# Output layer of one token block by seven half-size products for eight, with the retention stretches before it moved forward

## The chip, the cores and the metric

The kernel runs on one core of one Trainium2 chip. The metric is the device time of one execution in microseconds (us). Three runs of the kernel before gave a median of 314.52 us (314.04 to 317.05). The engines are named as in the profile: PE is TensorE's matmul side and PEld its weight load, DVE is VectorE, ACT is ScalarE, POOL is GpSimd, SP is SyncE, which here only issues DMAs.

## The reference

Two operators in a row. Retention over q, k and v of shape (batch 8, heads 8, sequence 576, head width 64), and a bilinear feed-forward layer on its output, with 4608 tokens of width 512 and an inner width of 1536:

```python
scores = scale * np.matmul(q, k.transpose(0, 1, 3, 2))
Dmat = np.where(rel >= 0, gamma[:, None, None] ** rel[None, :, :], 0.0)
attn = np.matmul(scores * Dmat[None], v)
x = attn.transpose(0, 2, 1, 3).reshape(B * S, H * D)
out = (x @ w_a) * (x @ w_b) @ w_out
```

Inputs and output are float32. The kernel multiplies in bfloat16 and sums in float32.

## The kernel before, in words

**Blocks.** The 4608 tokens go through the feed-forward layer in blocks of 512, 256, 256 and then seven of 512. A block has twelve hidden tiles F of 128 columns. For each F, `ffn_block` (line 1288) forms `pa` = x w_a (line 1324) and `pb` = x w_b (line 1345) in PSUM, four matmuls each; ACT copies `pa` to SBUF as `ha` (line 1338), DVE multiplies it with `pb` into the hidden tile `hT` (line 1350), which is called the gate here. When all twelve are there, the output layer `hT` w_out follows. The blocks from token 2048 on use seven products for eight in the hidden layer too (`middle_layer`, `last_layer`), which the change leaves alone.

**The two forms of the output layer.** The plain one (line 1371): for each of the four groups of 128 tokens, twelve matmuls of 512 columns into one PSUM tile `po`, then a copy by ACT or DVE to an output tile, put on the list `held`; `store_held` issues the DMA at a set place. The other form is `rows_mixed` (line 932), used by every block from token 1536 on: it splits rows, inner width and columns in two and needs seven half-size products for eight. Its 84 matmuls of 256 columns (line 972) read `hT`, `wo_sb`, the precomputed weight sums `wo_sums` (15 instructions of `weight_sums`, line 876) and row sums `hsum`, which DVE forms from `hT` (`row_sums`, line 889): five instructions over F 0 to 7, five over F 8 to 11; two of each five update `hT` in place. Its partial results lie in PSUM tiles `m340`, `m341`, `m15` (two banks, that of the retention's output tile `o`) and `m52`. ACT copies some of them (`straight`, `crossed`, line 984), POOL and DVE add them up (lines 996, 1006, 1013), and the next block stores them (`store_formed`, `store_mixed`). The order of the products is: ways 3 and 4 (24 matmuls), way 1 (12), then `cross` of the first half (12), which uses `m15`, `cross` of the second (12), which uses `m52`, and ways 6 and 7 (24).

**Retention.** It runs beside the feed-forward layer in units called pairs, 256 tokens each, numbered 0 to 17; pair n must be done before the block that reads its tokens. For a pair, SP loads q, k, v (`load_pair`, line 163), POOL casts and scales them (`ahead`, line 489), SP issues two transposing DMAs (`turn`, line 550) into `qkT`, and a `stretch(into, outof)` (line 772) puts on PE: outputs from the states of pair `outof`, the state sums `kv` of pair `into` (two PSUM banks of the pool `ps_ffn`, which has four and which `pa`, `pb`, `po` and the `m` tiles share), the scores of `into`, and the rest of the outputs of `outof`. The additions that free `kv` go to DVE (line 616), the copies of states and outputs to ACT (lines 619 to 627, 759). In the changed kernel's order on DVE the additions of an even pair stand behind the row sums that were issued before its stretch.

**Places.** The order is written by hand: the list `todo` (from line 1651) holds pairs of a place and a function; places count 512-column matmuls of the feed-forward layer, and a function is issued at the first edge (after a whole F, mostly) at or behind its place. `starts[n]` is the place at which the block of pair n begins. Small DVE jobs wait in `jobs` with a priority and are issued a few per F; ACT copies wait in `copies_due` and `later`. The block of tokens 1024 to 1535 begins at place 288 in both kernels. `MADE` holds the places of eight weight combinations (`combine`, line 1082) for the hidden layer of later blocks.

**Memory.** `stage` holds two buffers for each of q, k and v; a third for pairs 2, 5 and 8 lies in the pool `begin`, which is closed when the pools of `rows_mixed` (`hsum`, `straight`, `crossed`, `less`) open. `BY_HALVES` (line 1285) names six `pa` groups whose matmuls run as two of 256 columns.

Of the kernel before, what the change touches and what calls it, by code (L numbers as in the profile page):

```python
# [18 lines left out]
def kernel(  # L19
# [66 lines left out]
    h_pool = pool("hT", 1)  # L86
    ha_pool = pool("ha", 6)
    o_pool = pool("osb", 4)
    late, early = {}, ExitStack()
    begin = early.enter_context(tc.tile_pool(name="begin", bufs=1))  # L90
    ctx.push(early)

    def pools_mixed():

        if not late:
            early.close()
            for name, bufs in (("hsum", 1), ("straight", 2),
                               ("crossed", 2), ("less", 2),
                               ("combo", 1), ("rows", 1)):
                late[name] = early.enter_context(  # L100
                    tc.tile_pool(name=name, bufs=bufs))

# [979 lines left out]
    def combine(p, m, i):  # L1082

        pools_mixed()
        if (p, m) not in combos:
            shape = [128, 4, 2, 2, 128]
            if p in COMMON:
                both = late["combo"].tile([128, 2] + shape[1:], BF16,
                                          tag="combo", name="combos")
                combos[p, 0], combos[p, 1] = both[:, 0], both[:, 1]  # L1090
            else:
                combos[p, m] = stage.tile(shape, BF16, tag=("qf", "kf")[m],
                                          name="combo")
            for own in (0, 1):
                if (p, own) in combos:
                    combos[p + 1, own] = combos[p, own]
        (a11, a12), (a21, a22) = quarter_weights(m, p, 2)
        s3, s1, s2, s4 = (combos[p, m][:, k] for k in range(4))
        out, one, other, op = [(s3, a11, a21, ALU.subtract),
                               (s1, a21, a22, ALU.add),  # L1100
                               (s2, a22, s3, ALU.subtract),
                               (s4, a12, s2, ALU.subtract)][i]
        def made():
            nc.vector.tensor_tensor(out, one, other, op=op)

        jobs.append((1.5 + i / 10, 0.5, made))
# [2 lines left out]

    def combine_rows(tok0, i):  # L1110
        if tok0 not in row_combos:
            row_combos[tok0] = late["rows"].tile([128, 4, 2, 256], BF16,
                                                 tag="rows", name="rows")
# [136 lines left out]
    def last_layer(tok0, xT, hT, sums):  # L1250
# [31 lines left out]
            work(SHARE[way])  # L1282
        work(math.inf, 1)

    BY_HALVES = [(1024, F) for F in (4, 5, 6)] + [
        (256 * MIXED, F) for F in (8, 9, 10)]

    def ffn_block(tb, tok0, n, runs):

        xT = x_of(tok0, n)  # L1290
        hT = h_pool.tile([128, NF, 512], BF16, tag="h", name="hT")
        if tok0 >= 256 * MIXED:
            pools_mixed()
            sums = late["hsum"].tile([128, 3, NF // 2, 2, 128], BF16, tag="hsum",
                                  name="hsum")
# [9 lines left out]
        for count in runs:  # L1305
# [35 lines left out]
            for F in range(f0, f0 + count):  # L1341
# [8 lines left out]
                nc.vector.tensor_tensor(hT[:, F, 0:n], has[F][:, 0:n],  # L1350
                                        pb[:, 0:n], op=ALU.mult)
# [9 lines left out]
            f0 += count  # L1361
        if tb == 0:
            yield from rows_together(tok0, hT, (0, 1))
        if tok0 >= 256 * MIXED:
# [238 lines left out]
    for n in blocks:  # L1603
        for i in range(tok // 256, (tok + n) // 256):
            starts[i] = at
        at += total(n, tok >= 256 * MIXED) - 4 * (tok in MIDDLE)
        tok += n

    def early_casts():
# [34 lines left out]
    def third_turn():  # L1644
        for w in (Q, K):
            turned((4, w), (5, w))
        for i in (4, 5):
# [12 lines left out]
    todo += [(170, stretch, (3, None)), (201, stretch, (4, 3)),  # L1660
             (217, spread, ()),
             (252, stretch, (5, 4)), (274, open_alone, (5,)),
             (278, close_outputs, (5,)), (336, stretch, (6, None)),
             (372, stretch, (7, 6)), (408, stretch, (8, 7))]
    for n in range(8, NP, 2):
        todo += [(starts[n] - (92 if n == 16 else 116 if n > 8 else 112), stretch, (n + 1, n)),
                 (starts[n] - 52, stretch, (n + 2, n + 1))
                 if n + 2 < NP else
                 (starts[n] - 60, close_alone, (n + 1,))]
    placed = {args[0]: at for at, fn, args in todo if fn is stretch}  # L1670
# [3 lines left out]
             10: 412.2}  # L1674
    todo += [(116.1, load_pair, (4, (K, V))), (116.3, load_pair, (5,)),
             (141.5, load_pair, (6,)), (200.1, load_pair, (7, (Q, K))),
             (200.3, load_pair, (7, (V,))), (253.2, load_pair, (8, (Q,))),
             (253.3, store_held, (1,)), (253.4, load_pair, (8, (K,))),
             (253.5, store_held, (1,)), (253.6, load_pair, (8, (V,))),
             (253.7, store_held, (1,)), (283.2, load_pair, (9, (Q,))),  # L1680
             (283.3, store_held, (1,)), (283.4, load_pair, (9, (K, V))),
             (345, load_pair, (10, (Q,))), (380.1, load_pair, (10, (K,))),
             (380.2, store_held, (1,)), (380.3, load_pair, (10, (V,))),
             (380.4, store_held, (1,)), (411.9, load_pair, (11, (Q,))),
             (411.95, store_held, (2,)), (412.3, load_pair, (11, (K, V))),
             (458, load_pair, (12,)), (447, store_held, (2,)),
             (456, store_held, (2,))]
    NOW = 1, 4
    LATE = 30, 50, 8
    CAST_A, TURN_A, CAST_B, TURN_B = 96, 58, 96, 58  # L1690
# [51 lines left out]
```

## Time and profile before

| | |
|---|---|
| median of three runs | 314.52 us (314.04 to 317.05) |
| profiled execution | 313.77 us |
| its span | 312.1 us |
| PE busy | 301.7 us |
| DVE, POOL, ACT busy | 225.1, 201.9, 156.0 us |
| block of tokens 1024 to 1535 on PE | 85.86 to 120.44 us |
| block of tokens 1536 to 2047 on PE | 120.44 to 153.06 us |

The span is the time from the first to the last instruction of the profiled execution; the rest of its time lies around it. All times in the text are from the span's start. In a timeline row stand the start, the duration of the group, the engine, the line, the operation with its tiles (out<-in), and the count; in a group's row stand the busy time and the mean in ns of one. Matmuls overlap, so a group's duration includes the last one's way through the array: the pace is read from the starts. A few matmul records are missing from the trace; a group of 23 or 3 where the code issues 24 or 4 is such a case.

### The profile page before, as it was taken

How to read it: one execution, taken by the hardware profiler on the slowest of the kernel's cores; microseconds unless marked ns; L12 is line 12 of the kernel's file. 1: busy time of each engine (PE TensorE's matmuls, PEld its weight loads, DVE VectorE, ACT ScalarE, POOL GpSimd, SP SyncE). 2: the span in 40 equal slices, each digit the busy share in tenths (PEclk: the TensorE clock that was granted, in tenths of full speed). 3: DMA queues.
4: the chain of work that ended last, by engine and by line, in shares of the span. 5: the costliest groups of instructions: out<-in, count | busy, mean ns of one | idle time of the engine just before them, and what ended most of it. 6: DMA issues, size and time to landing. Idle time of an engine off the chain costs nothing.

```text
span 312.1 us, 9647 instructions
## 1 busy us (share of the span) xinstructions
PE 301.7 (97%) x3926; PEld 199.5 (64%) x3957; DVE 225.1 (72%) x452; ACT 156.0 (50%) x348; POOL 201.9 (65%) x288
## 2 busy tenths in 40 slices
PE   6899999999999999999999999999999999999995
PEld 2654457768555554567864787468746875687774
DVE  5944355768757685779777986888579968877873
ACT  6746346626435454555456545544635454335530
POOL 3980089675996679963799769985998350035413
PEclk9999999999999999999999999999999999999999
DMA  7999999998998999999999486837704020012004
GB/s 235 268 183 204 255 261 193 183 218 202 189 171 217 232 229 191 250 235 269 201 283 216 93 215 175 200 82 170 223 4 70 30 106 2 2 57 82 1 2 134
DMA packets 144797, 50.97 MB, mean 163 GB/s; under 512 B 126576, under 2 KB 141680, under 8 KB 144752
## 3 DMA queue, kind: packets, MB, share of 16 engines
q1 hardware_dynamic: 138272, 45.10, 63.3%
q0 software_dynamic: 5808, 4.72, 9.8%
q8 instruction: 31, 0.51, 0.7%
q10 hardware_dynamic: 672, 0.52, 0.5%
q14 instruction: 14, 0.11, 0.1%
HBM read 37.75 MB, written 9.44 MB: 151 GB/s over the span
## 4 chain that ended last, share of the span: by engine, by line
PE 91%; DMA 3%; DVE 2%; issue 1%; SPq 0%; POOL 0%; ACT 0%; POOLq 0%; DVEq 0%; ACTq 0%
PE m L972 16%; PE pb L1345 13%; PE pa L1324 12%; PE pb L1209 9%; PE pa L1209 9%; PE po L1371 8%; PE lm L1152 7%; PE ls L1152 3%; PE la L1152 2%; DMA wa_sb<-in_moe_w_a_dram 2%; PE po L858 2%; DMA vf<-in_v_dram 2%; PE sc L660 2%; PE o L688 1%; PE kv L589 1%
## 5 line engine op out<-in xcount | busy, mean ns | idle before, releaser
L1350 DVE TENSOR_TENSOR hT<-ha,pb 128x512 bf16<-128x512 bf16 (+1 forms) x60 | 34.5, 577 | 32.1 <-PE pb L1345 27.9
L1345 PE MATMUL pb<-xT,wb_sb 128*128 128x512 bf16 (+1 forms) x235 | 49.8, 335 | 0.4
L1324 PE MATMUL pa<-xT,wa_sb 128*128 128x256 bf16 (+1 forms) x252 | 47.7, 318 | 0.4 <-issue 0.3
L996 POOL TENSOR_TENSOR osb<-crossed,straight 128x256 f32<-128x256 f32 x24 | 17.5, 758 | 46.6 <-ACT crossed L984 46.6
L1338 ACT CAST ha<-pa 128x512 bf16<-128x512 f32 (+1 forms) x60 | 29.8, 500 | 35.4 <-PE pa L1324 34.2
L1324 PEld LDWEIGHTS <-wa_sb 128*128 128x128 bf16 x256 | 24.5, 98 | 16.0 <-DVE sums L616 0.2
L1345 PEld LDWEIGHTS <-wb_sb 128*128 128x128 bf16 x240 | 23.4, 98 | 17.1 <-issue 0.3
L541 POOL TENSOR_TENSOR vb<-vf,vs 128x512 bf16<-128x512 f32 x30 | 31.5, 1071 | 1.2
L1209 PE MATMUL pb<-xT,wb_sb 128*128 128x512 bf16 x125 | 32.1, 379 | 0.2
L1209 PE MATMUL pa<-xT,wa_sb 128*128 128x512 bf16 x119 | 31.4, 379 | 0.7 <-issue 0.3
L504 POOL TENSOR_TENSOR qkb<-qf,qs 64x512 bf16<-64x512 f32 x24 | 25.0, 1057 | 10.5 <-issue 4.7
L972 PEld LDWEIGHTS <-hT 128*128 128x128 bf16 x288 | 28.1, 98 | 5.0 <-DVE hT L906 0.5
L1219 ACT CAST ha<-pa 128x512 bf16<-128x512 f32 x32 | 18.7, 585 | 24.8 <-PE pa L1209 24.8
L1222 DVE TENSOR_TENSOR hT<-ha,pb 128x512 bf16<-128x512 bf16 x32 | 21.9, 684 | 10.4 <-PE pb L1209 6.7
L534 POOL CAST qkb<-kf 64x256 bf16<-64x256 f32 x60 | 27.3, 481 | 1.5
L1371 PE MATMUL po<-wo_sb,hT 128*128 128x512 bf16 x113 | 26.7, 379 | 0.8 <-issue 0.6
L509 POOL TENSOR_TENSOR qkb<-qf,qs 64x512 bf16<-64x512 f32 x24 | 26.1, 1107 | 0.7
L972 PE MATMUL m<-wo_sums,hsum 128*128 128x256 bf16 x216 | 25.7, 273 | 0.0
L530 POOL CAST qkb<-kf 64x512 bf16<-64x512 f32 x30 | 20.8, 694 | 5.0 <-DMA kf<-in_k_dram 3.6
L906 DVE TENSOR_TENSOR hsum<-hT 128x512 bf16<-128x512 bf16 (+2 forms) x51 | 23.1, 484 | 0.5
L972 PEld LDWEIGHTS <-hsum 128*128 128x128 bf16 x216 | 21.1, 98 | 2.5
L1209 PEld LDWEIGHTS <-wb_sb 128*128 128x128 bf16 x128 | 12.3, 98 | 14.3
(165 smaller groups left out, 577.3 us busy)
## 6 DMA issues: line engine op xcount, KB each, us to landing
qf<-in_q_dram SPq DMA_DIRECT2D x32, 256.0 KB, 4.5
vf<-in_v_dram SPq DMA_DIRECT2D x32, 256.0 KB, 4.3
kf<-in_k_dram SPq DMA_DIRECT2D x31, 256.0 KB, 4.2
out_dram<-osb SPq DMA_DIRECT2D x9, 512.0 KB, 3.6
out_dram<-osb SPq DMA_DIRECT2D x22, 128.0 KB, 2.7
wo_sb<-in_moe_w_out_dram POOLq DMA_DIRECT2D x3, 512.0 KB, 16.0
out_dram<-osb SPq DMA_DIRECT2D x6, 256.0 KB, 3.9
wa_sb<-in_moe_w_a_dram POOLq DMA_DIRECT2D x2, 512.0 KB, 8.3
```

The lines of the kernel that those rows point to most:

```text
L504: nc.gpsimd.tensor_tensor(per_head(qkb[0:64, Q])[:, hs], per_head(t[0:64])[:, hs], by[0:64, hs].unsqueeze(2).to_broadcast([64, H, D]), op= ...
L509: nc.gpsimd.tensor_tensor(per_head(qkb[64:128, Q])[:, 1 - r::2], per_head(t[64:128])[:, r::2], by[64:128, r::2].unsqueeze(2).to_broadcast( ...
L534: nc.gpsimd.tensor_copy(to[:, :, 1 - r], fro[:, :, r])
L541: nc.gpsimd.tensor_tensor(vb[:, e].rearrange("p (h d) -> p h d", d=D), t[:, e].rearrange("p (h d) -> p h d", d=D), decay[:, at], op=ALU.mult)
L972: nc.tensor.matmul(to, rows, cols, start=(begins and p == 0), stop=True, skip_group_check=True)
L1152: nc.tensor.matmul(to[:, m], w[:, c], x[:, c], start=(way in (1, 2, 5) and m == c == 0), stop=True, skip_group_check=True)
L1209: nc.tensor.matmul(p1, w[:, c, F * 128:F * 128 + 128], xT[:, c], start=(c == 0), stop=(c == NC - 1))
L1324: nc.tensor.matmul(pa[:, at:at + width], wa_sb[:, c, fs], xT[:, c, at:at + width], start=(c == at == 0), stop=(c == NC - 1), skip_group_ch ...
L1338: nc.scalar.copy(ha[:, 0:n], pa[:, 0:n])
L1345: nc.tensor.matmul(pb[:, 0:n], wb_sb[:, c, fs], xT[:, c], start=(c == 0), stop=(c == NC - 1))
L1350: nc.vector.tensor_tensor(hT[:, F, 0:n], has[F][:, 0:n], pb[:, 0:n], op=ALU.mult)
L1371: nc.tensor.matmul(po, hT[:, F, u * 128:(u + 1) * 128], wo_sb[:, F], start=(F == 0), stop=(F == NF - 1))
```

## The change

The output layer of the block of tokens 1024 to 1535 takes the form of `rows_mixed`: the tests on `256 * MIXED` (1536) become tests on `SQUARE` (1024). `store_mixed` gets a branch for pairs below 6, whose tokens lie in their natural order, and issues two DMAs of 128 rows for each. Since the pools of `rows_mixed` open 144 places sooner, the third staging buffers move from `begin` to a pool of their own, `extra`, which later also holds the combinations for which the pools `combo` and `rows` were opened. The stretches of pairs 6, 7 and 8 move from places 336, 372 and 408 to 316, 344 and 380, that of pair 10 from 52 to 48 places ahead of its block, in a block that is 6 places shorter; the loads and stores around them are put in another order, and `MADE` moves back. `BY_HALVES` becomes empty. On PE, stretch 6 now follows F = 3 of the block (before: F = 5), stretch 7 follows F = 6 (before: F = 10), stretch 8 follows F = 11 (before: half of the output layer), and stretch 10 follows F = 11 of its block (before: F = 10).

```diff
+    SQUARE = 1024
...
+    extra = pool("extra", 1)
...
-                               ("crossed", 2), ("less", 2),
-                               ("combo", 1), ("rows", 1)):
+                               ("crossed", 2), ("less", 2)):
...
-        extra = n < MIXED + 3 and n % 3 == 2
-        return (begin if extra else stage).tile(
+        third = n < MIXED + 3 and n % 3 == 2
+        return (extra if third else stage).tile(
...
         for kp, r0, m, b, s0 in rows_of(n):
+            if n < MIXED:
+                on.dma_start(out[b * S + s0:b * S + s0 + m, :], osb[:, kp])
+                continue
...
-    MADE = [385 + 8 * i for i in range(8)]
+    MADE = [400 + 9 * i for i in range(8)]
...
-            if p in COMMON:
-                both = late["combo"].tile([128, 2] + shape[1:], BF16,
-                                          tag="combo", name="combos")
...
+            combos[p, m] = combos[p + 1, m] = (
+                extra if p in COMMON else stage).tile(
+                    shape, BF16, tag=("qf", "kf")[m], name="combo")
...
-    BY_HALVES = [(1024, F) for F in (4, 5, 6)] + [
-        (256 * MIXED, F) for F in (8, 9, 10)]
+    BY_HALVES = []
...
-        if tok0 >= 256 * MIXED:
+        if tok0 >= SQUARE:
             pools_mixed()
...
-        if tok0 >= 256 * MIXED:
+        if tok0 >= SQUARE:
             yield from rows_mixed(tok0, hT, sums)
...
-             (278, close_outputs, (5,)), (336, stretch, (6, None)),
-             (372, stretch, (7, 6)), (408, stretch, (8, 7))]
+             (278, close_outputs, (5,)), (316, stretch, (6, None)),
+             (344, stretch, (7, 6)), (380, stretch, (8, 7))]
...
-                 (starts[n] - 52, stretch, (n + 2, n + 1))
+                 (starts[n] - (52 if n > 8 else 48), stretch, (n + 2, n + 1))
...
-             (200.3, load_pair, (7, (V,))), (253.2, load_pair, (8, (Q,))),
-             (253.3, store_held, (1,)), (253.4, load_pair, (8, (K,))),
-             (253.5, store_held, (1,)), (253.6, load_pair, (8, (V,))),
-             (253.7, store_held, (1,)), (283.2, load_pair, (9, (Q,))),
-             (283.3, store_held, (1,)), (283.4, load_pair, (9, (K, V))),
+             (200.3, load_pair, (7, (V,))), (253.05, load_pair, (8, (Q,))),
+             (253.3, load_pair, (8, (K, V))),
+             (283.2, store_held, (2,)), (283.3, load_pair, (9, (Q,))),
+             (283.4, store_held, (2,)), (283.5, load_pair, (9, (K, V))),
```

More of the change, by code (lines that the diff above doesn't have):

```diff
@@ L1086, in combine @@
             shape = [128, 4, 2, 2, 128]
-            if p in COMMON:
-                both = late["combo"].tile([128, 2] + shape[1:], BF16,
-                                          tag="combo", name="combos")
[L1090 to L1096, printed above, removed]
+            combos[p, m] = combos[p + 1, m] = (
+                extra if p in COMMON else stage).tile(
+                    shape, BF16, tag=("qf", "kf")[m], name="combo")
         (a11, a12), (a21, a22) = quarter_weights(m, p, 2)
@@ L1111, in combine_rows @@
         if tok0 not in row_combos:
-            row_combos[tok0] = late["rows"].tile([128, 4, 2, 256], BF16,
-                                                 tag="rows", name="rows")
+            row_combos[tok0] = extra.tile([128, 4, 2, 256], BF16,
+                                             tag="vf", name="rows")
         x = x_of(tok0, 512)
@@ L1363, in ffn_block @@
             yield from rows_together(tok0, hT, (0, 1))
-        if tok0 >= 256 * MIXED:
+        if tok0 >= SQUARE:
             yield from rows_mixed(tok0, hT, sums)
@@ L1605 @@
             starts[i] = at
-        at += total(n, tok >= 256 * MIXED) - 4 * (tok in MIDDLE)
+        at += total(n, tok >= SQUARE) - 4 * (tok in MIDDLE)
         tok += n
@@ L1676 @@
              (141.5, load_pair, (6,)), (200.1, load_pair, (7, (Q, K))),
-             (200.3, load_pair, (7, (V,))), (253.2, load_pair, (8, (Q,))),
-             (253.3, store_held, (1,)), (253.4, load_pair, (8, (K,))),
-             (253.5, store_held, (1,)), (253.6, load_pair, (8, (V,))),
-             (253.7, store_held, (1,)), (283.2, load_pair, (9, (Q,))),
-             (283.3, store_held, (1,)), (283.4, load_pair, (9, (K, V))),
-             (345, load_pair, (10, (Q,))), (380.1, load_pair, (10, (K,))),
[L1683 to L1687, printed above, removed]
+             (200.3, load_pair, (7, (V,))), (253.05, load_pair, (8, (Q,))),
+             (253.3, load_pair, (8, (K, V))),
+             (283.2, store_held, (2,)), (283.3, load_pair, (9, (Q,))),
+             (283.4, store_held, (2,)), (283.5, load_pair, (9, (K, V))),
+             (345, load_pair, (10, (Q,))), (380.1, load_pair, (10, (K,))),
+             (380.2, store_held, (2,)), (380.3, load_pair, (10, (V,))),
+             (380.4, store_held, (2,)), (411.9, load_pair, (11, (Q,))),
+             (412.3, load_pair, (11, (K, V))),
+             (452, load_pair, (12,))]
     NOW = 1, 4
```

## The prediction

> **What bounds the kernel now.** I read the page first: TensorE's share, its granted clock, the chain that ended last.
>
> ```profile
> span 312.1 us, 9647 instructions
> ...
> PE 301.7 (97%) x3926; PEld 199.5 (64%) x3957; DVE 225.1 (72%) x452; ACT 156.0 (50%) x348; POOL 201.9 (65%) x288
> ...
> PEclk9999999999999999999999999999999999999999
> ...
> PE 91%; DMA 3%; DVE 2%; issue 1%; SPq 0%; POOL 0%; ACT 0%; POOLq 0%; DVEq 0%; ACTq 0%
> ```
>
> TensorE is busy for 97% of the span at full clock and holds 91% of the chain. Then I asked for the busy times in three stretches: the block of tokens 1024 to 1535, the block of 1536 to 2047, and the rest.
>
> ```profile
> 85.86:120.44 34.58, 34.16 (x466) 18.05 (x468) 23.60 (x43) 17.37 (x34) 26.09 (x35) 1.00 1.01 206
> 120.44:153.06 32.62, 32.30 (x437) 20.97 (x440) 25.36 (x45) 15.52 (x30) 22.83 (x30) 1.00 1.07 235
> 153.06:312.10 159.04, 154.00 (x1904) 109.83 (x1915) 122.33 (x251) 76.75 (x157) 98.99 (x128) 1.00 0.44 110
> ```
>
> The columns are the stretch, its length, then busy time of PE, PEld, DVE, ACT and POOL. In the two blocks that the change touches PE idles for 0.42 and 0.32 us. So the time moves one for one with TensorE's work there, and there is next to no wait to win back.
>
> **The change part by part.** First the products of the last layer of the block of 1024, from the timeline of PE (start, duration, operation):
>
> ```profile
> 108.70 5.34 PE L1371 MATMUL po<-wo_sb,hT 128*128 128x512 bf16 x24
> ...
> 115.47 5.13 PE L1371 MATMUL po<-wo_sb,hT 128*128 128x512 bf16 x23 [0.16 <-issue]
> 120.44 1.03 PE L1324 MATMUL pa<-xT,wa_sb 128*128 128x512 bf16 x4
> ```
>
> The last layer of the block of 1536, from the busy times of line 972 alone (the stretch, its length, PE and PEld):
>
> ```profile
> 143.86:153.06 9.20, 9.20 (x84) 8.10 (x83) 1.00 1.12 194
> ```
>
> Starts, not durations, give the pace. The second `po` group runs 4.97 us to 120.44 and shows 23 products: 0.216 us each, and one record of 24 is missing (the "issue" gap of 0.16 is that record, no idle time). The block's 48 full-width products therefore take 48 x 0.216 = 10.37 us, and the retention stretch between them takes (120.44 - 108.70) - 10.37 = 1.37. The block of 1536 already does the new form: 84 products of 256 columns in 9.20 us without a gap, 0.1095 each. **The saving is 10.37 - 9.20 = 1.17 us.** The Trainium skill, "TensorE: Matmul & The Clock Gate", section "Back-to-back issue gap", speaks against it: a stream of weight loads and matmuls is to sustain about 131 ns per matmul at 512 columns and 81 at 128, so that a half width costs far more than half; by it, with some 98 ns (an estimate between the two) at 256, 48 x 0.131 = 6.3 us would become 84 x 0.098 = 8.2, a loss of 1.9 us. The rows above, 216 and 110 ns, don't agree with it.
>
> Next the products in halves (`BY_HALVES`): three in each of the two blocks.
>
> ```profile
> 91.04 1.03 PE L1324 MATMUL pa<-xT,wa_sb 128*128 128x512 bf16 x4
> 91.91 1.03 PE L1345 MATMUL pb<-xT,wb_sb 128*128 128x512 bf16 x4
> 92.77 1.04 PE L1324 MATMUL pa<-xT,wa_sb 128*128 128x256 bf16 x8
> 93.64 1.03 PE L1345 MATMUL pb<-xT,wb_sb 128*128 128x512 bf16 x3
> ...
> 96.34 0.45 PE L589 MATMUL kv<-vb,qkb 64*64 64x64 bf16 x32
> ...
> 96.98 1.05 PE L1324 MATMUL pa<-xT,wa_sb 128*128 128x256 bf16 x8
> 97.86 1.03 PE L1345 MATMUL pb<-xT,wb_sb 128*128 128x512 bf16 x3
> ```
>
> A full product group takes 91.91 - 91.04 = 0.87, one in halves 0.87 to 0.88; six cost 0.06 us too much at most. **Saving 0.06.**
>
> Moving the stretches of pairs 6, 7 and 8 forward changes no PE work. But it places stretch 8 (and 10, by the 48 for 52) directly behind the last hidden product of its block and ahead of the 84 products. The sums that these products need are made on VectorE, and here lies the one wait that I find. Stretch 8 takes two of the four PSUM banks (`kv0`, `kv1`); the two after them go to `m340`, `m341`; the seventh tile, `m52`, gets kv0's bank, and its first product waits until VectorE has added kv0 up. That addition stands in VectorE's queue behind the row sums:
>
> ```profile
> L1350 DVE TENSOR_TENSOR hT<-ha,pb 128x512 bf16<-128x512 bf16 x36 | 24.6, 686 | 26.6 <-PE pb L1345 25.1 <-ACT ha L1338 1.5
> L906 DVE TENSOR_TENSOR hsum<-hT 128x1024 bf16<-128x1024 bf16 x12 | 10.9, 904 | 0.3
> L906 DVE TENSOR_TENSOR hT<-hT 128x1024 bf16<-128x1024 bf16 x8 | 7.0, 912 | 0.0
> L906 DVE TENSOR_TENSOR hsum<-hT 128x512 bf16<-128x512 bf16 x21 | 7.8, 416 | 0.0
> L906 DVE TENSOR_TENSOR hT<-hT 128x512 bf16<-128x512 bf16 x14 | 5.4, 416 | 0.0
> L613 DVE COPY sums<-kv 128x256 f32<-128x256 f32 x5 | 2.1, 413 | 0.0
> L616 DVE TENSOR_TENSOR sums<-kv,sums 128x256 f32<-128x256 f32 x44 | 18.6, 422 | 1.6
> ```
>
> Let T be the end of the last hidden product (block start 85.86, 24 groups of 4 x 0.216, stretch 6 at 96.98 - 96.34 = 0.6 or a little more, stretch 7 as long as stretch 8: about 108.6). VectorE then does in order, by the mean durations: the gate 0.686, one wide sum 0.904, two wide updates 1.824, three sums 1.248, two updates 0.832, the copy 0.413 and two additions 0.844: T + 6.75. PE comes to `m52` after stretch 8 (1.37) and 48 products (5.26): T + 6.63. I take a **wait of 0.12 us**. The ends: 0, since back to back these operations start up to a tenth closer than they last; and 2.2, if all three wide ones take their longest and the gate before (line 10 of 12) is late:
>
> ```profile
> L906 DVE TENSOR_TENSOR hsum<-hT x51: 276/416/1345, 136.6 to 302.1; 128x512 bf16<-128x512 bf16 x21, 128x256 bf16<-128x256 bf16 x18, 128x1024 bf16<-128x1024 bf16 x12
> L906 DVE TENSOR_TENSOR hT<-hT x34: 279/416/1527, 141.7 to 302.5; 128x512 bf16<-128x512 bf16 x14, 128x256 bf16<-128x256 bf16 x12, 128x1024 bf16<-128x1024 bf16 x8
> ```
>
> That is 0.44 + 2 x 0.61 more than the means. The late gate I estimate at 0.5: ScalarE's state copies of stretch 7 come to stand just ahead of the copy that the gate of F = 10 needs, and two of them last this long:
>
> ```profile
> 109.60 1.24 ACT L619 CAST states<-sums 64x512 bf16<-64x512 f32 x2
> ```
>
> In the block of 1536 one wide update, not two and a wide sum, stands behind the last gate, so kv0 is free 0.904 + 0.912 sooner, 1.7 us before `m52`: no wait.
>
> What is new beside it costs nothing so long as its cover holds.
>
> ```profile
> L1104 DVE TENSOR_TENSOR combos<-wa_sb,combos 128x512 bf16<-128x512 bf16 x2 | 1.8, 908 | 0.0
> L996 POOL TENSOR_TENSOR osb<-crossed,straight 128x256 f32<-128x256 f32 x24 | 17.5, 758 | 46.6 <-ACT crossed L984 46.6
> 128.40 2.04 POOL L541 TENSOR_TENSOR vb<-vf,vs 128x512 bf16<-128x512 f32 x2
> ```
>
> VectorE gains ten row sums in the first block (6.6 us by the means above) and hands weight combinations (`MADE`), of 0.9 us at most, to the next; the windows leave it 11.0 and 7.3 us idle. ScalarE makes four copies for two and is idle for half the window. POOL gains four additions of 0.76 us, which lie between the casts of pairs 9 and 10, so that those of pair 10 end at 130.4 + 3.0 = 133.5. Stretch 10 needs them at T + 1.4 + 9.3 + 20.7 + 1.4, about 141.4; if that cover went, PE would wait us for us. The held output copies go; the block's stores are still four of 256 KB, issued by the next block; `extra` takes over the third staging buffers and the combinations, with the reuse that they had.
>
> The moved stretches need their transposed queries and keys sooner. From the SP and POOL timelines and the transposes' time to landing:
>
> ```profile
> 82.83 3.62 SPq L558 DMA_TRANSPOSE qkT<-qkb  x2
> 86.50 1.74 SPq L171 DMA_DIRECT2D vf<-in_v_dram  x2
> 88.72 4.41 SPq L558 DMA_TRANSPOSE qkT<-qkb  x2
> ...
> 103.16 1.35 SPq L558 DMA_TRANSPOSE qkT<-qkb  x1
> ```
>
> ```profile
> 91.12 0.75 POOL L534 CAST qkb<-kf 64x256 bf16<-64x256 f32 x2
> ```
>
> ```profile
> DMA to landing us min/median/max: 2.7/3.6/7.1
> ```
>
> Stretch 6 now starts after line 3, at 85.86 + 8 x 0.864 = 92.8; its transposes are issued by 86.5 and, at the median, have landed by 90. Stretch 7 starts after line 6, at 92.8 + 0.7 + 5.2 = 98.7; its second transpose waits for the cast that ends at 91.9, is issued by 93.1 even with the one load that now goes ahead, and lands by about 96.7. Stretch 8 starts at 108.6; its transposes, issued at 103.16 and after, move ahead of the stores, so not later, and land by about 108. The slack is 2 us at the first two and about 1 at the third: no cost. SP then issues eight stores around pair 9's query load where two stood behind it, which puts its keys and values about 1 us later; stretch 9 comes 1.1 us sooner but more than 17 us after T.
>
> The sum: -1.17 - 0.06 + 0.12 = **-1.11 us**. The profiled execution took 313.77 us (span 312.1 and 1.67 around it), so 312.66; it lay 0.75 below the median of the three runs, 314.52, and on that median the forecast is **313.4**.
>
> **The rivals.**
>
> 1. *VectorE holds the bank (slower).* The row sums run beside POOL's multiplications for pair 9, and `m52` waits 2.2 us instead of 0.12: -1.23 + 2.2 = +0.97, 315.5. It decides from a wait of 1.23 us, that is, the second addition on kv0 ending after T + 7.9. For it: the two longest L906 rows, which are twice the means. Against: POOL stands idle until pair 9's queries land, about when the updates run. The Trainium skill, "SBUF — State Buffer", section "Who interferes with whom", has it that a VectorE instruction with two SBUF inputs and a GpSimd one that reads SBUF exclude each other for a whole instruction; the spread of 0.68 to 1.53 us for the same 1024-wide sums agrees with that.
>
> 2. *A transpose is late.* If one of stretch 7 takes the longest landing, 7.1 us, and the load ahead of it adds 1 us, it lands at 93.1 - 1.25 + 7.1 + 1.0 = 99.95, 0.7 after PE wants it: -1.11 + 0.7, 314.1. The neighbours' rows, at 3 to 4 us, speak against it.
>
> 3. *The change doesn't do what it says*: 84 half-width products cost in this block what 48 full ones do, 0.123 each. That gives 314.5 and is refuted next door, unless weights read from fresh sums load slower here.
>
> 4. *More is won*: no wait at `m52`, and 0.3 of the 0.74 us of idle time goes too: -1.53, 313.0.
>
> **How the numbers follow.** Forecast 0.66; rival 1 0.14; rival 2 0.09; rival 3 0.04; rival 4 0.07. The range starts at the fastest run shown, 314.04, less 1.53, 312.5, and ends at rival 1, 315.5. Within 1% (3.1 us, what a measurement of this kernel can tell from no change) lie all cases: 0.94. Faster by over 1% would need 2 us more than all work that goes: 0.02. Slower by over 1% needs rivals 1 and 2 together at several times their price: 0.04.
>
> **What would show it.** In the changed profile the block from its first `pa` should take 34.6 - 1.1 = 33.5 us, with 84 `m` products at 0.11 us and one gap of 0 to 0.3 us ahead of the 49th, released by VectorE's additions. No idle time of PE should be released by a transpose at stretches 6 to 8. The block of 1536 should shrink by 0.03 and everything behind 153 stay as it was, only 1.1 us earlier. The prediction is wrong if that gap exceeds 1 us, if PE waits for `qkT`, if `m` products run slower than 0.11 us, or if the later blocks wait for POOL's shifted casts.

## The result and the profile after

The changed kernel takes 317.12 us (median of nine runs, 316.35 to 319.33) where the kernel before takes 314.81 beside it (314.04 to 317.05). The ratio is 1.0083 with a 95% interval of 1.0060 to 1.0107: slower by about 2.6 us. Forecast was a gain of 1.1. Ratios here and below leave out executions in which the chip was disturbed, so they are not the quotients of the medians. The profiled execution took 317.05 us; its page first:

```profile
span 315.3 us, 9724 instructions
...
PE 304.6 (97%) x3969; PEld 201.2 (64%) x3969; DVE 237.3 (75%) x466; ACT 156.8 (50%) x350; POOL 206.3 (65%) x292
...
PE 84%; DVE 7%; DMA 3%; ACT 2%; issue 1%; SPq 0%; POOL 0%; DVEq 0%; ACTq 0%; POOLq 0%
```

PE's share of the chain falls from 91 to 84% and DVE's rises from 2 to 7%. (PE's busy time can't be compared: this trace lacks fewer matmul records.) The same three stretches as before, cut at the first matmul of each block (length, busy time of PE, PEld, DVE, ACT, POOL):

```profile
85.86:123.13 37.27, 34.35 (x494) 20.34 (x493) 29.95 (x49) 18.34 (x36) 29.09 (x37) 1.00 1.07 206
123.13:156.28 33.15, 32.76 (x430) 19.87 (x428) 30.50 (x55) 15.43 (x30) 24.64 (x32) 1.00 1.05 230
156.28:315.30 159.02, 155.01 (x1918) 109.85 (x1915) 122.64 (x251) 76.75 (x157) 99.04 (x128) 1.00 0.43 108
```

Everything ahead of 85.86 and behind token 2048 lasts as long as before (159.02 and 159.04). The loss is in the two blocks: 37.27 for 34.58 and 33.15 for 32.62, together +3.22 us. PE's timeline shows where:

```profile
107.90 1.03 PE L1341 MATMUL pb<-xT,wb_sb 128*128 128x512 bf16 x4
...
110.42 2.79 PE L976 MATMUL m<-wo_sums,hT 128*128 128x256 bf16 x24
113.05 1.04 PE L976 MATMUL m<-wo_sums,hsum 128*128 128x256 bf16 x8
115.31 0.61 PE L976 MATMUL m<-wo_sums,hsum 128*128 128x256 bf16 x4 [1.22 <-DVE hsum L907]
115.76 0.60 PE L976 MATMUL m<-wo_sb,hT 128*128 128x256 bf16 x4
117.13 1.14 PE L976 MATMUL m<-wo_sb,hT 128*128 128x256 bf16 x8 [0.77 <-DVE hT L907]
119.20 1.47 PE L976 MATMUL m<-wo_sb,hT 128*128 128x256 bf16 x12 [0.93 <-DVE sums L617]
120.51 2.78 PE L976 MATMUL m<-wo_sums,hsum 128*128 128x256 bf16 x24
123.13 1.03 PE L1320 MATMUL pa<-xT,wa_sb 128*128 128x512 bf16 x4
...
128.00 1.02 PE L1341 MATMUL pb<-xT,wb_sb 128*128 128x512 bf16 x4 [0.39 <-DVE hT L1346]
```

T, the end of the last hidden product, is 107.90 + 4 x 0.216 = 108.76. The 84 products run from 110.42 to 123.13, 12.71 us, and PE stands still three times: for the row sums that way 1 still lacks, for the updates of `hT` that follow them, and for the addition that frees `m52`'s bank. Read from the starts the three gaps come to 3.5 us (the listed waits, 2.92, count from modelled ends). Without them the products would take 12.71 - 3.5 = 9.2 us, as forecast. Stretch 8 lasts 110.42 - 108.76 = 1.66 where it lasted 1.37. A fourth wait stands at the third `pb` of the next block. What PE waits for is all on VectorE:

```profile
109.12 0.68 DVE L1346 TENSOR_TENSOR hT<-ha,pb 128x512 bf16<-128x512 bf16 x1
109.72 1.44 DVE L907 TENSOR_TENSOR hsum<-hT 128x1024 bf16<-128x1024 bf16 x1
111.08 2.98 DVE L907 TENSOR_TENSOR hT<-hT 128x1024 bf16<-128x1024 bf16 x2
113.99 2.55 DVE L907 TENSOR_TENSOR hsum<-hT 128x512 bf16<-128x512 bf16 x3
116.46 1.36 DVE L907 TENSOR_TENSOR hT<-hT 128x512 bf16<-128x512 bf16 x2
117.75 0.41 DVE L614 COPY sums<-kv 128x256 f32<-128x256 f32 x1
118.27 1.34 DVE L617 TENSOR_TENSOR sums<-kv,sums 128x256 f32<-128x256 f32 x3
```

VectorE works without a pause from the last gate on and does what the prediction lists, in that order, but the second of the last three additions ends at about 119.1, T + 10.4 and not T + 6.75. The gate, the copy and the additions take their usual times. The eight row sums don't. POOL at the same time:

```profile
109.57 2.48 POOL L505 TENSOR_TENSOR qkb<-qf,qs 64x512 bf16<-64x512 f32 x2 [5.22 <-PE o L689]
112.11 2.86 POOL L510 TENSOR_TENSOR qkb<-qf,qs 64x512 bf16<-64x512 f32 x2
```

It stands idle for 5.22 us until 109.57 and then multiplies for pair 9, just when the row sums begin to take about twice their time. (The two wide sums of 106.68 and 108.52, while POOL was idle, took 0.68 us.)

### The profile page after: what moved, and what is told of

Its sections match the earlier page's. It is cut to its first block, busy times and chain, and to the rows that moved or that the text cites. A ratio compares the mean times of both kernels' runs of the same rounds, so it can differ in the third digit from the quotient of the medians.

```text
span 315.3 us, 9724 instructions
## 1 busy us (share of the span) xinstructions
PE 304.6 (97%) x3969; PEld 201.2 (64%) x3969; DVE 237.3 (75%) x466; ACT 156.8 (50%) x350; POOL 206.3 (65%) x292
## 4 chain that ended last, share of the span: by engine, by line
PE 84%; DVE 7%; DMA 3%; ACT 2%; issue 1%; SPq 0%; POOL 0%; DVEq 0%; ACTq 0%; POOLq 0%
PE m L976 16%; PE pb L1341 12%; PE pa L1320 11%; PE pa L1206 9%; PE pb L1206 9%; PE lm L1149 7%; PE po L1367 5%; PE ls L1149 3%; DVE hsum L907 2%; DVE hT L907 2%; DMA wa_sb<-in_moe_w_a_dram 2%; PE la L1149 2%; PE po L859 2%; PE sc L661 1%; DMA vf<-in_v_dram 1%
## 5 line engine op out<-in xcount | busy, mean ns | idle before, releaser
L1000 POOL TENSOR_TENSOR osb<-crossed,straight 128x256 f32<-128x256 f32 x28 | 20.1, 746 | 49.5 <-ACT crossed L988 45.1
L1320 PE MATMUL pa<-xT,wa_sb 128*128 128x512 bf16 (+1 forms) x232 | 48.2, 335 | 0.0
L976 PEld LDWEIGHTS <-hT 128*128 128x128 bf16 x336 | 32.4, 98 | 7.7 <-DVE hT L907 1.7
L1341 PEld LDWEIGHTS <-wb_sb 128*128 128x128 bf16 x240 | 23.4, 98 | 18.8 <-issue 1.0
L1320 PEld LDWEIGHTS <-wa_sb 128*128 128x128 bf16 x232 | 22.2, 98 | 17.1 <-DVE sums L617 0.5
L976 PE MATMUL m<-wo_sums,hsum 128*128 128x256 bf16 x252 | 30.1, 273 | 1.2 <-DVE hsum L907 1.2
L907 DVE TENSOR_TENSOR hsum<-hT 128x512 bf16<-128x512 bf16 (+2 forms) x57 | 29.3, 546 | 0.5
L976 PEld LDWEIGHTS <-hsum 128*128 128x128 bf16 x252 | 24.6, 98 | 4.3 <-DVE hsum L907 1.5
L976 PE MATMUL m<-wo_sb,hT 128*128 128x256 bf16 x168 | 20.2, 273 | 1.9 <-DVE hT L907 1.0
L1149 PEld LDWEIGHTS <-combo 128*128 128x128 bf16 x192 | 18.8, 98 | 4.7
```

The costliest lines, as they stand in the source:

```text
L907: lambda e=ways[i]: nc.vector.tensor_tensor(*e[:3], op=e[3]))
L976: nc.tensor.matmul(to, rows, cols, start=(begins and p == 0), stop=True, skip_group_check=True)
L1149: nc.tensor.matmul(to[:, m], w[:, c], x[:, c], start=(way in (1, 2, 5) and m == c == 0), stop=True, skip_group_check=True)
L1320: nc.tensor.matmul(pa[:, at:at + width], wa_sb[:, c, fs], xT[:, c, at:at + width], start=(c == at == 0), stop=(c == NC - 1), skip_group_ch ...
L1341: nc.tensor.matmul(pb[:, 0:n], wb_sb[:, c, fs], xT[:, c], start=(c == 0), stop=(c == NC - 1))
```

## The experiments

Three theories are tried. The names e1 to e11 are those that the expectations use; the changed kernel's second run is a1. **A**: the row sums, which read two operands from SBUF, are slowed by POOL's work for pair 9. **B**: VectorE's queue behind the last gate is too long by itself. **C**: the moved stretches and loads cost the time. All variants start from the changed kernel. Profiled executions differ by up to 1.8 us in the part ahead of the block of 1024, which is nearly the same code in all (it begins at 85.64 to 87.41), so profiles are compared from the block's start: "two blocks" is from there to the first product of the block of 2048. The changed kernel itself takes 70.42 us there in one profile and 70.04 in the next, so single profiles can't tell apart differences of 0.4 us.

**The changed kernel once more, beside other runs (a1).**

> The changed kernel as it is, on the chip and beside the runs of the following three. All theories: ratio to the kernel before 1.006 to 1.011; 12.7 us from the first of the 84 products to the end of the block; wide row sums of 1.4 to 1.5 us beside POOL's multiplications for pair 9.

Ratio 1.0103 (1.0074 to 1.0132), waits of 0.62, 0.78 and 0.92, two blocks 70.04 us, 12.1 us for the 84 products and not 12.7. The loss and its place repeat; the waits' sizes differ by some tenths between executions.

**Pair 9's query load behind all eight stores (e1).**

```diff
-             (283.2, store_held, (2,)), (283.3, load_pair, (9, (Q,))),
-             (283.4, store_held, (2,)), (283.5, load_pair, (9, (K, V))),
+             (283.2, store_held, (2,)), (283.3, store_held, (2,)),
+             (283.4, load_pair, (9, (Q,))), (283.5, load_pair, (9, (K, V))),
```

> Edit: the query load of pair 9 is issued on SP behind all eight held stores and no longer between them, so that POOL's ten instructions for pair 9 start some 3 us later, at about 112.5 us. Theory A (the row sums on DVE are slowed because POOL's pair 9 runs beside them): those row sums that now end before POOL starts take 0.68 us (1024 wide) and 0.42 us (512 wide), the three waits of PE inside the 84 products (3.5 us by the starts) fall below 1.2 us in sum, the kernel takes about 314.8. Theory B (DVE's queue behind the last gate is too long by itself): the waits stay where they are with 3 us or more, about 317. Theory C (the moved stretches and loads cost it, whatever the products): about 317 as well.

Ratio 1.0055 (1.0029 to 1.0080). PE still waits 1.72 and 0.93 us (3.1 in sum by the starts), and the two blocks take 70.02 us, no less than in a1. VectorE's and POOL's timelines of this kernel:

```profile
110.80 1.29 DVE L907 TENSOR_TENSOR hT<-hT 128x1024 bf16<-128x1024 bf16 x2
112.00 3.63 DVE L907 TENSOR_TENSOR hsum<-hT 128x512 bf16<-128x512 bf16 x3
115.56 2.01 DVE L907 TENSOR_TENSOR hT<-hT 128x512 bf16<-128x512 bf16 x2
```

```profile
111.47 2.69 POOL L505 TENSOR_TENSOR qkb<-qf,qs 64x512 bf16<-64x512 f32 x2 [8.77 <-DMA qf<-in_q_dram]
114.22 2.32 POOL L510 TENSOR_TENSOR qkb<-qf,qs 64x512 bf16<-64x512 f32 x2
```

POOL starts 2.2 us behind T (109.24 here), where it started 0.8 behind it, and the border in VectorE's rows moves with it. The two wide updates, which took 1.45 each in the changed kernel, are now ahead of POOL and take 0.6. The narrow ones, half as wide, fall beside POOL and take 1.2 each. The gain expected of it did not come, because the slow part only moved to other instructions; but the mechanism of theory A is visible. A sum beside POOL's multiplications takes about as long as one of them (1.2 to 1.4 us here), whether it is 512 or 1024 wide.

**POOL's work for pairs 9 and 10 taken out of the window (e5)**, and stretch 9 made 32 places later (80 for 112; the expectation says 36), so that it can wait for them.

```diff
-        todo += [(starts[n] - (92 if n == 16 else 116 if n > 8 else 112), stretch, (n + 1, n)),
+        todo += [(starts[n] - (92 if n == 16 else 116 if n > 8 else 80), stretch, (n + 1, n)),
...
-    casts = {3: 116, 4: 116.15, 5: 141, 6: 200, 7: 253, 8: 283, 9: 376,
-             10: 412}
-    turns = {3: 116, 4: 116.2, 5: 141.2, 6: 200.2, 7: 253.1, 8: 283.1, 9: 380,
-             10: 412.2}
+    casts = {3: 116, 4: 116.15, 5: 141, 6: 200, 7: 253, 8: 283, 9: 425,
+             10: 425.4}
+    turns = {3: 116, 4: 116.2, 5: 141.2, 6: 200.2, 7: 253.1, 8: 283.1, 9: 425.2,
+             10: 425.6}
...
-             (412.3, load_pair, (11, (K, V))),
+             (425.8, load_pair, (11, (K, V))),
```

> Edit: POOL's casts of pairs 9 and 10 and their transposes are issued behind the block's 84 products, stretch 9 goes 36 places back; POOL is idle while the row sums of the block of tokens 1024 are formed. Theory A (row sums slowed by POOL): every row sum there takes its shortest, 0.68 or 0.42 us, the additions that free kv0 end by T + 6.2 (T the end of the last hidden product), PE waits under 0.4 us in sum inside the 84 products, which take 9.2 to 9.6 us from first to last instead of 12.7. Theory B (DVE's queue is too long by itself): 11.5 us or more. The kernel's whole time is not the question, since pairs 9 and 10 come late; where that costs nothing, A gives 313.7, B 316.5.

POOL is idle from 103.4 to 117.3. VectorE's and PE's timelines:

```profile
110.23 1.28 DVE L907 TENSOR_TENSOR hT<-hT 128x1024 bf16<-128x1024 bf16 x2
111.44 1.09 DVE L907 TENSOR_TENSOR hsum<-hT 128x512 bf16<-128x512 bf16 x3
112.44 0.75 DVE L907 TENSOR_TENSOR hT<-hT 128x512 bf16<-128x512 bf16 x2
113.11 0.42 DVE L614 COPY sums<-kv 128x256 f32<-128x256 f32 x1
113.63 1.34 DVE L617 TENSOR_TENSOR sums<-kv,sums 128x256 f32<-128x256 f32 x3
```

```profile
110.19 2.79 PE L976 MATMUL m<-wo_sums,hT 128*128 128x256 bf16 x24
...
119.37 1.03 PE L1320 MATMUL pa<-xT,wa_sb 128*128 128x512 bf16 x3
```

The same instructions in the same order, and the 84 products take 9.18 us without a wait. The second addition ends at about 114.5, T + 5.8. So B is refuted: the queue is short enough when POOL is still. A is shown. The DMAs that moved along are not the cause: in the changed kernel the transposes of pair 9 are issued from 116.99 on, 7 us after the first slow sum, and pair 11's loads later still. As a whole this kernel is slower still, ratio 1.0152 (1.0132 to 1.0171): in the block of 1536 the additions of the late stretch 9 come to stand behind five wide row sums, which run beside POOL's late work for pair 10 (134.86 to 139.28), and PE waits 2.78 us for them. POOL's work has to be done somewhere. The Trainium skill, "SBUF — State Buffer", section "Who interferes with whom", says that a VectorE instruction with two SBUF inputs and a GpSimd one that reads SBUF exclude each other for a whole instruction. These rows and those of e1 agree: 0.33 us per narrow sum alone (start to start) and 1.2 beside POOL.

**The plain output layer kept, with all the moves (e3).**

```diff
-    SQUARE = 1024
+    SQUARE = 256 * MIXED
...
-             (452, load_pair, (12,))]
+             (452, load_pair, (12,)), (447, store_held, (2,)),
+             (456, store_held, (2,))]
```

> Edit: the output layer of the block of tokens 1024 goes back to the eight full-width products, everything else of the change stays (stretches, loads, MADE, no halves); four held stores are put back at places 447 and 456. Theories A and B (the row sums are late): no wait of PE above 0.2 us between 100 and 120 us, the two blocks take 67.1 to 67.7 us together as against 67.2 before, the kernel 314.8 to 315.3. Theory C (the moves cost it): the two blocks take more than 68.5 us, the kernel 316 or more.

Ratio 1.0027 (1.0006 to 1.0048). PE waits for nothing in either block, and they take 34.67 + 32.78 = 67.45 us:

```profile
86.36:121.03 34.67, 34.30 (x454) 17.03 (x456) 23.21 (x41) 17.38 (x34) 27.59 (x37) 1.00 0.95 199
121.03:153.81 32.78, 32.52 (x428) 19.93 (x429) 25.30 (x47) 15.43 (x30) 21.08 (x28) 1.00 1.01 234
```

That is 0.25 more than before (67.20), with no wait that names a cause. C can answer for this much, not for the 3.2.

**Stretch 8 one F earlier (e4)**, so that the additions of its `kv` banks stand ahead of the narrow sums.

```diff
-             (344, stretch, (7, 6)), (380, stretch, (8, 7))]
+             (344, stretch, (7, 6)), (372, stretch, (8, 7))]
```

> Edit: stretch 8 goes one hidden tile forward, place 372 for 380. If its place right ahead of the products is the cause (PSUM banks held by its state sums), the wait ahead of the 49th product goes and the waits in sum fall from 3.5 to 2.3 us or less, the kernel to 316. If the row sums are the cause (A or B), they now stand behind the additions of stretch 8 and its 1.4 us of cover is gone: the 49th product no longer waits on additions, the waits on row sums grow by 1.3 to 2.5 us, and the kernel takes 317 to 318.5.

Ratio 1.0185 (1.0138 to 1.0233), worse than expected. PE's longest wait, and VectorE ahead of it:

```profile
116.18 3.15 PE L976 MATMUL m<-wo_sums,hT 128*128 128x256 bf16 x14 [3.73 <-DVE hT L1346]
```

```profile
109.34 2.94 DVE L907 TENSOR_TENSOR hsum<-hT 128x1024 bf16<-128x1024 bf16 x2
112.21 2.99 DVE L907 TENSOR_TENSOR hT<-hT 128x1024 bf16<-128x1024 bf16 x2
...
115.45 0.67 DVE L1346 TENSOR_TENSOR hT<-ha,pb 128x512 bf16<-128x512 bf16 x1
```

The stretch empties the list of small jobs into VectorE's queue, so that four wide sums come to stand ahead of the gate of F = 11. Beside POOL they take 1.45 each, and now the gate itself is late. The 84 products take 15.7 us, 6.5 more than without waits; some 2.6 of these lie behind the long wait, as gaps inside its group and the next. The 49th product no longer waits, so the banks that stretch 8 holds are not what costs the time: with them free the loss is larger. The order of that queue thus decides what the slowdown costs, not only its amount.

**The combinations later (e2)**, out of the places inside the products, where nothing can be issued and they pile up ahead of the next block's gates.

```diff
-    MADE = [400 + 9 * i for i in range(8)]
+    MADE = [427 + 8 * i for i in range(8)]
```

> Edit: MADE starts at place 427 with a step of 8, so that no weight combination stands ahead of the first gates of the block of tokens 1536. If the three combinations there are what holds that block's third pb group, its gap of 0.56 us goes and the block takes 32.6 us, 0.5 less; the kernel 316.6. If DVE is late there for what it carries over from the row sums, the gap stays at 0.3 or more and the time at 317.1. The three waits inside the 84 products stay in either case.

Ratio 1.0080 (1.0054 to 1.0107). The wait at the third `pb` is gone, the three waits in the products stay (0.65, 0.78, 0.93), two blocks 69.84. But the block of 1536 takes 32.91 us, 0.24 less than 33.15 and not the 0.5 expected: two combinations now stand ahead of stretch 9's additions, and PE loses about 0.3 at a `pa` behind that stretch. The combinations also read two operands from SBUF. In the changed kernel the three ahead of the gates took 2.9 us beside POOL's work for pair 10 (124.40 to 127.27); in e9 below, with POOL idle, they take 0.34 each from start to start. So this wait too has the slowdown of theory A in it.

**More row sums per gate (e6 with the late query load, e7 without).** The block of 1024 may issue 1.5 us of small jobs behind each gate instead of 1.0, so that fewer sums are left for the time beside POOL; the combinations are later as above. With the query load late as well, and without:

```diff
-                work(1.0)
+                work(1.5 if tok0 == SQUARE else 1.0)
```

> Edit: three at once. The DVE jobs issued per hidden tile of the block of 1024 may cost 1.5 for 1.0, so that four of the five wide row sums stand ahead of the gate of F = 10 and all five ahead of that of F = 11; MADE starts at 427; pair 9's query load behind all held stores. Theory A: the wide sums run while POOL idles (104 to 111 us), the small ones at 0.42 to 1.2; PE waits 0 to 0.6 us inside the products, none at the third pb of the next block; the time is 313.5 to 314.2, under the kernel before. Theory B: the queue behind the last gate is shorter by 2.8 us of wide sums, so most waits go as well, 314 to 314.8: A and B are told apart by the next run. If the wide sums ahead of the gates make the gates late, a wait moves to the pb groups, and the time stays above 315.5.

> Edit: the former without the move of pair 9's query load, so POOL starts that pair at about 109.5, beside the small row sums and perhaps the last wide one. Theory A: 0.5 to 1.5 us longer than the former, the difference lying in row sums beside POOL's multiplications. Theory B: the same time as the former within 0.3.

With the late load: ratio 1.0036 (1.0018 to 1.0054), the 84 products 111.70 to 120.88, 9.18 us without a wait; two blocks 67.10, with one wait of 0.67 at a `pa` of the second, because two combinations stand ahead of stretch 9's additions. Without it: 1.0017 (1.0002 to 1.0031), one wait of 0.52 in the products, two blocks 67.37. Of the 3.2 us lost in the two blocks, 3.3 and 3.0 come back, so that they take about what they took before (67.20): the gain of the products is there, and the waits that are left eat it. Theory A had e7 0.5 to 1.5 us longer than e6. In the block of 1024 it is, 34.41 for 33.65, but its next block is 0.5 shorter, and the ratios, whose intervals overlap, point the other way.

**The combinations split around stretch 9**, again without (e8) and with the late load (e9), from the kernel of the last two runs.

```diff
-    MADE = [427 + 8 * i for i in range(8)]
+    MADE = [427, 435, 443, 468, 476, 484, 492, 500]
```

> As e7 (row sums allowed 1.5 us a gate in the block of 1024, combinations later), but the fourth combination and those behind it stand behind stretch 9 (places 468 to 500). If what was left of the loss in e7 is POOL's pair 9 beside the narrow sums (theory A: one wait of 0.5 ahead of the 49th product) and combinations ahead of stretch 9's additions (0.2 to 0.7): the two blocks take 66.9 to 67.3 us (e7 67.37, before 67.20), from the block's start to the end 226.0 to 226.4, the time 314.3 to 314.8, the same as before. If the rest of the loss is something of the moves (e3 paid 0.25 us with no wait): 314.8 to 315.2 as e7.

> As the run beside it, with pair 9's Q load behind all eight stores, so that POOL's first multiplication starts about 111.5 and the narrow sums end beside less of it. Under theory A there is no wait in the 84 products (9.2 us) and none at the first pa of the block's neighbour: two blocks 66.2 to 66.6 us, 225.6 to 226.0 to the end, the time 313.8 to 314.2, some 0.5 us less than before. If the moves cost by themselves: 314.6 to 315.4 as e6 and e7.

Both missed: 1.0031 (1.0010 to 1.0052) and 1.0048 (1.0027 to 1.0068), two blocks 67.79 and 67.66 where 66.2 to 67.3 were expected. The first waits 0.15 and 0.81 in the products of the block of 1024. The second has the block of 1024 as forecast, and loses the gain in the next one:

```profile
86.49:119.95 33.46, 33.46 (x493) 20.50 (x492) 25.85 (x50) 18.45 (x36) 23.93 (x34) 1.00 0.94 197
119.95:154.15 34.20, 32.95 (x431) 19.80 (x429) 29.83 (x49) 15.43 (x30) 26.02 (x32) 1.00 1.02 223
```

```profile
143.93 2.78 DVE L907 TENSOR_TENSOR hsum<-hT 128x512 bf16<-128x512 bf16 x3
...
147.30 0.75 DVE L1101 TENSOR_TENSOR combo<-wb_sb 128x512 bf16<-128x512 bf16 x2
147.98 0.87 DVE L1101 TENSOR_TENSOR combo<-wb_sb,combo 128x512 bf16<-128x512 bf16 x2
```

The block of 1024 takes 33.46 us, 1.12 less than before. In the block of 1536 the narrow sums now meet POOL's values of pair 11 (143.41 to 146.1), the four combinations left for the end come behind them, and PE waits 0.98 at the 49th product: the same collision, one block on.

**No combination ahead of the second block's additions; 1.5 us per gate in the later blocks of `ffn_block` too (e10 and e11).** Both with the late query load. The first has one combination ahead of the next block's first gates and one ahead of stretch 9's additions, against the kernel just shown:

```diff
-                work(1.5 if tok0 == SQUARE else 1.0)
+                work(1.5 if tok0 >= SQUARE else 1.0)
...
-    MADE = [427, 435, 443, 468, 476, 484, 492, 500]
+    MADE = [421, 427, 435, 443, 458, 464, 470, 476]
```

The second has two ahead of the gates and none ahead of the additions, against the first:

```diff
-    MADE = [421, 427, 435, 443, 458, 464, 470, 476]
+    MADE = [421, 423, 427, 435, 458, 464, 470, 476]
```

> Row sums allowed 1.5 us a gate in both blocks, pair 9's Q load behind the eight stores, combinations at places 421 to 443 (one of them ahead of the first gates, one ahead of stretch 9's additions) and 458 to 476, so that none stands ahead of the block of 1536's state additions. If theory A with its consequence on VectorE's queue is the whole cause: no wait in either block's products, at most 0.3 us at the pa behind stretch 9; two blocks 66.0 to 66.5 us (before 67.20), to the end 225.3 to 226.0, the time 313.5 to 314.2 beside 314.4. If something else of the change costs time by itself: two blocks near 67 and 314.8 to 315.5, as in e6 and e7.

> As the run beside it, with two combinations ahead of the first gates (about 1.5 us of VectorE while PE works on the first two pa and pb) and none between the third and fourth gate, so that stretch 9's additions are not held up. Theory A: no wait at the pa behind stretch 9, two blocks 65.9 to 66.2 us, the time 313.3 to 314.0; the price is a wait at the third pb of up to 0.3 us if two combinations ahead of the gates are already too many (with three it was 0.5). If something else costs: 314.8 to 315.5.

Ratios 1.0019 (0.9993 to 1.0044) and 1.0019 (0.9997 to 1.0040): no difference from before that these runs resolve. Neither kernel waits in the products of the block of 1024, and they have that block at 33.36 and 33.51; in the block of 1536 the first loses some 0.3 us within its products, the second nothing. But now the wide sums of the second block run beside POOL (from 135.00 to 140.4 it multiplies for pair 11), between the gates. VectorE's and PE's timelines of the first kernel:

```profile
135.32 2.71 DVE L907 TENSOR_TENSOR hsum<-hT 128x1024 bf16<-128x1024 bf16 x2
137.95 0.68 DVE L1346 TENSOR_TENSOR hT<-ha,pb 128x512 bf16<-128x512 bf16 x1
```

```profile
141.60 1.02 PE L1341 MATMUL pb<-xT,wb_sb 128*128 128x512 bf16 x4 [1.03 <-DVE hT L1346]
...
143.34 0.44 PE L590 MATMUL kv<-vb,qkb 64*64 64x64 bf16 x31 [0.32 <-DVE hT L1346]
```

The gates come late and PE waits for them, 1.03 and 0.32 us; in the second kernel 0.76, 0.58 and 0.53. Two blocks 67.95 and 68.60, not the 65.9 to 66.5 expected of theory A alone.

So no variant beats the kernel before. The gain of the products is there in every run that has no wait in that block's products (blocks of 1024 of 33.36 to 33.65 us for 34.58), but no run had a clean second block along with it. What also stays open: the 0.25 us of the moves alone, and the differences between a run's two blocks and its ratio, up to 1.2 us either way (e6: 0.1 us less than before in the two blocks, 1.1 us more by the ratio).

## Why the prediction was wrong

**The products (-1.17): right.** 9.18 us for 84 wherever nothing holds them; rival 3, that they would run slower here, is out.

**The halves (-0.06): right as far as it can be seen.** The hidden products of the changed kernel run at 0.864 us a group.

**The wait at `m52` (+0.12, ends 0 and 2.2): the step that failed.** The order of VectorE's queue and the releaser at `m52` were right; the term was mis-sized, because VectorE's row sums were priced at their groups' means, without POOL's work beside them. The waits measured 3.5 us, in three parts, beyond even the upper end. Against the prediction's durations, from the starts in VectorE's timeline: the two wide updates 2.91 for 1.824, the three narrow sums 2.47 for 1.248, the two narrow updates 1.29 for 0.832, the wide sum done 0.73 late, together 3.5 us. The narrow sums were priced at their mean of 0.416, and even the upper end stretched only the wide ones. The rows of before hold the reason why that mean was worth little. VectorE's narrow sums of the block of 1536 there, and POOL:

```profile
146.10 1.09 DVE L906 TENSOR_TENSOR hsum<-hT 128x512 bf16<-128x512 bf16 x3
147.10 0.75 DVE L906 TENSOR_TENSOR hT<-hT 128x512 bf16<-128x512 bf16 x2
```

```profile
140.96 2.49 POOL L541 TENSOR_TENSOR vb<-vf,vs 128x512 bf16<-128x512 f32 x2
149.99 0.77 POOL L996 TENSOR_TENSOR osb<-crossed,straight 128x256 f32<-128x256 f32 x1 [6.54 <-ACT crossed L984]
```

POOL is idle from 143.5 to 150, so nothing of POOL ran beside these sums, and they last just what the mean says. In the new place POOL is in the middle of a pair. What that costs stood in the kernel before as well, at POOL's multiplications for the same pair 9:

```profile
111.44 1.26 DVE L1104 TENSOR_TENSOR combos<-wa_sb,combos 128x512 bf16<-128x512 bf16 x1
```

```profile
111.12 2.47 POOL L504 TENSOR_TENSOR qkb<-qf,qs 64x512 bf16<-64x512 f32 x2 [4.68 <-issue]
```

This combination, 512 wide with two operands in SBUF like a narrow sum, took 1.26 us. The other one of its group took 0.55, and the prediction shows the two only as their mean of 908 ns.

**Only the last of three deadlines was checked.** Way 1 needs the narrow sums, and the next 12 products the updates, before `m52` needs its bank. By the prediction's own durations the narrow sums end at T + 4.66, and PE wants the last of them at T + 1.37 + 32 x 0.1095 = T + 4.87; the slack was 0.2 us there too. That changes where PE stands, not how long in all: the last deadline sets the sum (T + 10.4, less stretch 8 of 1.66 and 48 products of 5.26, is 3.5).

**Rival 1 was the case, and its price and its counter-argument failed.** Its mechanism, row sums beside POOL's multiplications for pair 9, is the one that the runs show, and its deciding point, T + 7.9, was passed (T + 10.4). It was held off by "POOL stands idle until pair 9's queries land, about when the updates run". That is nearly so, and no argument against it: POOL started at 109.57, just ahead of the last wide sum, and all eight sums behind the last gate ran beside it. A chance of 0.14 was too little for a case in which the new instructions fall into a stretch that the rows of before show POOL to be busy in, and its price of 2.2 us stretched the three wide ones alone.

**Costs put at nothing.** The weight combinations were not hidden: three of them stand ahead of the next block's first gates, and PE loses 0.56 us there by the starts; the run that moves them has no wait there and one of 0.3 behind stretch 9. The transposes were in time: PE waits for none at stretches 6 to 10, so rival 2 is out. Pair 10's later casts made no one wait. Stretch 8 was to keep its 1.37 and took 1.66; in the variants it takes 1.37 to 1.65 and in a1 1.76, and the cause stays open. The block of 1536 was to shrink by 0.03 and grew by 0.53, which is the wait behind the combinations. Behind it nothing changed, as predicted.

**The account.** Block of 1024: products 9.18 - 10.37 = -1.19, waits in them +3.53, stretch 8 +0.29, the rest +0.06: +2.69. Block of 1536: +0.53. Together +3.22 in the profiled execution, and about 2.6 by the ratio.

## What to carry to other kernels

When an edit adds VectorE instructions with two SBUF operands, lay POOL's timeline beside their new place first, and price them there from rows that ran beside POOL, not by the group's mean: the same row sum took 0.33 us alone and 0.8 to 1.2 beside POOL. In these runs the price was about 0.85 us per instruction beside POOL's multiplications, for 512 columns (1.2 less 0.33) and for 1024 (1.45 less 0.60), so a chain of short ones suffers most. And where PE consumes a chain step by step, work out the slack at each step, since a hand-placed order with slacks of 0.2 us turns any slowdown of the producer into a wait.

## What was not expected of the hardware

A narrow sum beside POOL can take as long as a wide one: 1.2 us each for 512 columns with the load late, 1.45 for 1024 columns in the changed kernel; alone 0.33 and 0.60 from start to start. Instructions of VectorE that take one operand from PSUM kept their durations beside POOL (the gate 0.68, the additions on `kv` 0.42 each). POOL is slowed as well: in the changed kernel its two multiplications of line 510 took 2.86 us beside the sums (112.11), and 2.06 where VectorE ran none (96.42).
